# Softmax attention and a spectral filter in one kernel: some exponentials move from ScalarE to VectorE, and the instruction streams are list-scheduled anew

## The chip, the cores and the metric

The kernel runs on one core of a Trainium2 chip. The metric is the time of one execution on the device in microseconds (us), the median of several runs. An engine name in short: PE is TensorE (matmuls; PEld its weight loads), ACT is ScalarE, DVE is VectorE, POOL is GpSimd, SP is SyncE, which only issues transfers.

## What is computed

Two independent results are laid side by side in the output: multi-head attention of `A_x`, and a two-dimensional real Fourier filter of `B_x`. All inputs are bf16.

```python
B, S, D = 1, 2048, 448
H = 16; Dh = D // H                        # 16 heads of 28
q, k, v = split(x @ wqkv)                  # wqkv: D x 3D
p = softmax(q @ k.T * Dh ** -0.5)          # per head: 2048 x 2048
a = (p @ v) @ wo                           # 2048 x 448

X = rfft2(x.astype(float32))               # S x 225 complex
y = irfft2(X * (w_r + 1j * w_i), s=(S, D)) # 2048 x 448
out = concatenate([a, y], axis=-1)
```

The attention needs 16 x 2048 x 2048 exponentials, which is 1024 *units* of 128 x 512 (128 keys on the partitions, 512 queries in the columns). The Fourier transforms are products with constant tables of cosines and sines.

## The kernel before

Heads are handled in four groups of four. The 28 numbers of each head lie in a strip of 32 partitions, so the scores of different heads run in different row strips of the array at the same time, and the four products of the probabilities with V run in four column strips. A unit `u` is one head `j`, one block of 128 keys `kc`, one block of 512 queries `qc`, one group `g`. Three units make one exp of 128 x 1536. PSUM has eight banks of 512 fp32 columns: six for scores (two triples), one accumulator (`ACC`), one for all other products ("jobs").

```python
def emit_st(t):                      # scores of three units
    for u in us:
        e.matmul(bank(u % 6), kT[32*j:32*j+28, ...], qT[32*j:32*j+28, ...],
                 start=True, stop=True, tile_position=(32 * j, 0))          # L649
def emit_act(t):
    e.activation(ET[:, t % NE, 0:n], PS[:, b0:b0 + n], ACT.Exp, scale=scale) # L659
def emit_pv(u0):                     # four heads, one block of keys
    e.matmul(ACC[32*j:32*j+32, :], Vaug[:, g % 2, kc, 32*j:32*j+32],
             ET[...], start=(kc == 0), stop=(kc == 15),
             tile_position=(0, 32 * j))                                      # L670
```

`Vaug` has a column of ones beside the 28 of V, so the accumulator also holds the sums of the softmax; after 16 blocks of keys they are turned, inverted, spread and multiplied in (`finish`). Projections for the next group (L393 for q and k, L408 for v), the output product (L711) and the spectral half are jobs: lists of full-array matmuls into bank 7, each ended by a copy out of PSUM, mostly on VectorE.

```python
def s_job(h, r, b):   # along S: 8 matmuls of 112 x 512, table F1 (1024 rows)   L464
def x_job(h,sg,r,b):  # along D: 8 matmuls of 113 x 512                        L487
def zmul(b, sg, h):   # times the filter: 6 products and sums and a copy on GpSimd, 113 x 512
def w_job(q,part,b):  # the filter's tables turned on TensorE                   L534
def y_job(t, r):      # back along D: 8 matmuls of 128 x 448                    L554
def z_job(a, odd):    # back along S: 8 matmuls of 128 x 448                    L586
```

A loop of Python decides at build time in which order each engine gets its instructions; it keeps an estimate of when each engine is free (`P.free`) and emits, at each step, a scores pass if its banks are free, else a V product, else a job's next matmul. Each engine then runs its own list strictly in that order and waits on semaphores.

Of the kernel before, what the change touches and what calls it, by code (L numbers as in the profile page):

```python
# [10 lines left out]
F32 = mybir.dt.float32  # L11

_ENG = ("sp", "act", "pe", "dve", "pool")
LAT = 0.12


class Prog:

    def __init__(self, nc, sems):
        self.nc = nc
        self.streams = {e: [] for e in _ENG}
        self.sems = sems
        self.count = {name: 0 for name in sems}
        self.wm = {e: {name: 0 for name in sems} for e in _ENG}
        self.trk = {}
        self.csem = {"act": "act", "pe": "pe", "dve": "dve", "pool": "pool"}
        self.dma_sems = set(n for n in sems if n.startswith("d_"))
        self.free = {e: 0.0 for e in _ENG}  # L30
        self.dma_free = 0.0
        self.tw = {}
        self.tr = {}

# [11 lines left out]
    def _emit_waits(self, eng, reads, writes):  # L46
        waits = {}

        def add(ev):
            if ev is None:  # L50
                return
            s, v = ev
            if s in self.dma_sems:
                v = self.count[s]
            if eng == "pe" and s == "pe":
                return
            if self.wm[eng][s] >= v:
                return
            if waits.get(s, 0) < v:
                waits[s] = v  # L60
        for k in reads:
            add(self._entry(k)["w"])
# [10 lines left out]
    def _mark(self, eng, ev, reads, writes, end):  # L73
# [3 lines left out]
        for k in writes:  # L77
            en = self._entry(k)
            en["w"] = ev
            en["r"] = []  # L80
            self.tw[k] = (eng, end)

    def ready(self, eng, reads=(), writes=()):

        t = 0.0
        for k in list(reads) + list(writes):
            w = self.tw.get(k)
            if w is not None and w[0] != eng:
                t = max(t, w[1] + LAT)
        for k in writes:  # L90
            for r, e in self.tr.get(k, {}).items():
                if r != eng:
                    t = max(t, e + LAT)
        return t

    def op(self, eng, fn, reads=(), writes=(), cost=0.1, tail=0.15):
        self._emit_waits(eng, reads, writes)
        sem = self.csem[eng]
        self.count[sem] += 1
        ev = (sem, self.count[sem])  # L100
        semh = self.sems[sem]
        self.streams[eng].append(lambda e, fn=fn, semh=semh: fn(e).then_inc(semh, 1))
        start = max(self.free[eng], self.ready(eng, reads, writes))
        self.free[eng] = start + cost
        self._mark(eng, ev, reads, writes, start + cost + tail)
        return start + cost

    def dma(self, eng, fn, sem, reads=(), writes=(), kb=128, issue=0.6):
        self._emit_waits(eng, reads, writes)
# [6 lines left out]
        self.dma_free = max(self.dma_free, start + issue) + kb / 280.0  # L116
        self._mark("dma", ev, reads, writes, self.dma_free + 2.0)

# [18 lines left out]
S = 2048  # L137
# [4 lines left out]
KBN = (113, 112)  # L142


def spectral_constants():


    s = np.arange(1024)
    f1 = np.zeros((4, 128, 8, 512))
    f2 = np.zeros((8, 128, 2, 8, 128))  # L150
    for h in range(2):
        k = 2 * np.arange(512) + h
        ang = 2 * np.pi * ((s[:, None] * k[None, :]) % S) / S
        re = np.cos(ang)
        im = -np.sin(ang)
        if h == 0:
            im[:, 0] = (-1.0) ** s
        for part, m in enumerate((re, im)):
            f1[2 * h + part] = m.reshape(8, 128, 512).transpose(1, 0, 2)
            mt = m.T.reshape(4, 128, 8, 128)  # L160
            f2[:, :, part, 4 * h:4 * h + 4, :] = mt.transpose(2, 1, 0, 3)
    d = np.arange(D)
# [3 lines left out]
    t1 = np.stack([c, sn, -sn, -c]).reshape(4, 4, 112, KD).transpose(2, 0, 1, 3)  # L166
    cf = np.full(KD, 2.0)
    cf[0] = cf[224] = 1.0
    c2 = (cf[None, :] * c / (S * D)).T
    s2 = (cf[None, :] * sn / (S * D)).T  # L170
    t2 = np.zeros((128, 4, 2, D))
    for v, m in enumerate((c2, -s2, s2, -c2)):
        for b in range(2):
            t2[0:KBN[b], v, b, :] = m[KB0[b]:KB0[b] + KBN[b], :]
    return f1, f2, t1, t2


def build_kernel(nc, A_x, A_wqkv, A_wo, B_x, B_w_r, B_w_i, out):
    NG = 4
    UN = 1024  # L180
    TU = 3
    NT = (UN + TU - 1) // TU
    NE = 5
    WARM = 20
    scale = float(DH) ** -0.5
    bf16np = mybir.dt.np(BF16)

    f1, f2, t1, t2 = spectral_constants()
    cst = np.zeros((128, 3, 128), np.float32)
    cst[:, 0, :] = np.eye(128)  # L190
    cst[:, 1, :] = np.eye(128)[::-1]
    for j in range(4):
        cst[32 * j + DH, 2, j] = 1.0
    f1_h = nc.inline_tensor(f1.reshape(4 * 128, 4096).astype(bf16np), name="cst_f1")
    f2_h = nc.inline_tensor(f2.reshape(8 * 128, 2048).astype(bf16np), name="cst_f2")
    t1_h = nc.inline_tensor(t1.reshape(112, 16 * KD).astype(bf16np), name="cst_t1")
    t2_h = nc.inline_tensor(t2.reshape(128, 8 * D).astype(bf16np), name="cst_t2")
    cst_h = nc.inline_tensor(cst.reshape(128, 384).astype(bf16np), name="cst_id")

    ctx = ExitStack()  # L200
    with ctx:
        sem_names = ["pe", "act", "dve", "pool"]
        sem_names += ["d_x%d" % i for i in range(3)] + ["d_w", "d_wv", "d_wo", "d_c", "d_t1", "d_t2", "d_xb"]
        sem_names += ["d_f%d" % i for i in range(4)] + ["d_wb%d" % i for i in range(2)] + ["d_o%d" % i for i in range(4)]
# [5 lines left out]
        wst = sb("wst", [128, 4, 1344])  # L210
# [3 lines left out]
        qT = sb("qT", [128, 2, S])  # L214
        kT = sb("kT", [128, 2, S])
        Vaug = sb("Vaug", [128, 2, 16, 128])
        ET = sb("ET", [128, NE, 1536])
        oaug = sb("oaug", [128, 2, 512])
        rz = sb("rz", [128, 2, 16])
        rzrep = sb("rzrep", [128, 2, 512])  # L220
        onrm = sb("onrm", [128, NG, S])
        cid = sb("cid", [128, 3, 128])
        astg = sb("astg", [128, 4, 448])
        R1 = sb("R1", [128, 10752])
        R2 = sb("R2", [128, 8192])
        WT = sb("WT", [128, 2, 2, 2, 1024])
        Wst = sb("Wst", [128, 2, 2, 4, KD])
        FR = sb("FR", [128, 2, 4096])
        T1 = sb("T1", [128, 4, 4, KD])
        T2 = sb("T2", [128, 4, 2, 448])  # L230
        ptmp = sb("ptmp", [128, 2, 512], F32)
        Esb = sb("Esb", [128, 2, 448], F32)
        PS = ctx.enter_context(nc.psum_tensor("PS", [128, 4096], F32))
        ACC = PS[:, 3072:3584]

        xb = R1[:, 0:7168].rearrange("p (c d) -> p c d", c=16)
        xs = R1[:, 7168:10752].rearrange("p (c d) -> p c d", c=8)
        X = R1[:, 0:8192].rearrange("p (b s r k) -> p b s r k", b=2, s=2, r=2)
        Sd = R2[:, :].rearrange("p (b r k) -> p b r k", b=4, r=2)
        Y = R2[:, 0:7168].rearrange("p (t r d) -> p t r d", t=8, r=2)  # L240
        F1v = FR[:, :, :].rearrange("p i (c m) -> p i c m", c=8)
        F2v = FR[:, :, :].rearrange("p i (j r t s) -> p (i j) r t s", j=2, r=2, t=8)

        crow = [(0, 128, 0), (0, 128, 128), (0, 128, 256), (64, 128, 320)]

        xa = R2[:, 0:1792].rearrange("p (c d) -> p c d", c=4)
# [4 lines left out]
        def copy(eng, dst, src, reads, writes, cost):  # L251
            if eng == "act":
                P.op("act", lambda e: e.activation(dst, src, ACT.Copy), reads=reads, writes=writes, cost=cost)
            else:
                P.op(eng, lambda e: e.tensor_copy(dst, src), reads=reads, writes=writes, cost=cost)  # L255


        P.dma("sp", lambda e: e.dma_start(cid[:, :, :], cst_h.ap()[:, :].rearrange("p (i k) -> p i k", i=3)), "d_c", writes=["cid"], kb=96)
        P.dma("sp", lambda e: e.dma_start(xa, A_x[0][0:512, :].rearrange("(c p) d -> p c d", p=128)),
              "d_x0", writes=["xa"], kb=448)  # L260
        for lo, hi, sem, key in ((0, 896, "d_w", "w"), (896, 1344, "d_wv", "wv")):
            P.dma("act", lambda e, lo=lo, hi=hi: e.dma_start(wst[:, 0:3, lo:hi], A_wqkv[0:384, lo:hi].rearrange("(c p) k -> p c k", p=128)),
                  sem, writes=[(key, 0)], kb=0.75 * (hi - lo))
            P.dma("act", lambda e, lo=lo, hi=hi: e.dma_start(wst[64:128, 3, lo:hi], A_wqkv[384:448, lo:hi]),
                  sem, writes=[(key, 1)], kb=0.125 * (hi - lo))
        for n, lo, hi in ((1, 512, 1024), (2, 1024, 2048)):
            for c in range(4):
                dlo = crow[c][2]
                P.dma("sp", lambda e, lo=lo, hi=hi, c=c, dlo=dlo: e.dma_start_transpose(xAT[:, c, lo:hi], A_x[0][lo:hi, dlo:dlo + 128]),
                      "d_x%d" % n, reads=["xa"], writes=[("xAT", n, c // 2)] + ([("xAT", 3, c // 2)] if n == 2 else []), kb=(hi - lo) / 2, issue=1.2 * n)  # L270

        P.op("dve", lambda e: e.memset(onrm[:, 0, 0:512], 0.0), writes=["zero"], cost=0.3)
        P.op("dve", lambda e: e.memset(wk[:], 0.0), writes=["wk0", "wk"], cost=1.0)
        P.op("dve", lambda e: e.memset(wq[:], 0.0), writes=["wq0", "wq"], cost=1.0)
        P.op("pool", lambda e: e.memset(wo[:], 0.0), writes=["wo"], cost=1.6)
        for i in range(2):
            P.op("pool", lambda e, i=i: e.memset(Vaug[:, i, :, :], 0.0), writes=[("V", i, n) for n in range(4)], cost=1.9)
# [620 lines left out]
```

The softmax here doesn't subtract the row's maximum and nothing guards it: scores larger than these inputs give would overflow.

## Time and profile before

| | before |
|---|---|
| median of 3 runs | 563.34 us (560.5 to 572.84) |
| span of the profiled run | 570.4 us |
| mean granted clock of TensorE | 0.844 |
| exps on ScalarE (L659), busy | 467.3 us, 342 instructions |
| idle of ScalarE before exps | 79.0 us |
| TensorE busy / VectorE busy / GpSimd busy | 500.1 / 132.4 / 87.1 us |

The page divides the span into 40 slices and gives each engine's busy share in tenths, and the clock that TensorE was granted, also in tenths (9 is 90% or more). Groups of instructions are named by their source line (L659), engine, output and inputs. "Idle before" is the time an engine stood still just ahead of a group, with what ended the wait. A busy TensorE at half clock does half the work, so its busy time has to be read beside the clock.

### The profile page before, as it was taken

The numbers are of one execution on the slowest core, as the hardware profiler recorded it, in microseconds if no ns is written. First come the engines' busy times: TensorE is split into PE (matmuls) and PEld (weight loads), VectorE is DVE, ScalarE is ACT, GpSimd is POOL, SyncE is SP. The second block draws the span as 40 slices with busy tenths as digits, with TensorE's granted clock in tenths as the row PEclk, the third lists the DMA queues.
The fourth block names the chain that finished last, engine by engine and source line by source line (L and its number), as shares of the span: only waits on it lengthen the run. The fifth ranks groups of instructions, "written<-read, shape, count | busy, mean of one in ns | idle before, by whom it ended". The sixth has DMA issues, their size and how long they took to land.

```text
span 570.4 us, 7748 instructions
## 1 busy us (share of the span) xinstructions
PE 500.1 (88%) x3276; PEld 164.7 (29%) x3276; DVE 132.4 (23%) x218; ACT 473.6 (83%) x352; POOL 87.1 (15%) x87
## 2 busy tenths in 40 slices
PE   7699795999999999989999899999978888788786
PEld 3222232223333233333333222222222222222222
DVE  2111332212212222122211211213132122222323
ACT  2667895869999999999988579889977559899894
POOL 5038000000000000582505555000000000000000
PEclk9555755659999999999968659789999669999999
DMA  6492130000022022000000000000000011301012
GB/s 167 87 302 81 43 95 16 2 1 0 1 75 75 2 72 75 1 0 2 1 1 0 1 0 1 2 0 1 1 0 1 1 53 55 106 17 41 24 34 80
DMA packets 21394, 21.69 MB, mean 38 GB/s; under 512 B 11792, under 2 KB 19472, under 8 KB 20848
## 3 DMA queue, kind: packets, MB, share of 16 engines
q1 hardware_dynamic: 20208, 19.60, 11.8%
q10 hardware_dynamic: 960, 1.20, 0.7%
q0 software_dynamic: 192, 0.40, 0.3%
q8 instruction: 25, 0.41, 0.3%
q14 instruction: 9, 0.07, 0.1%
HBM read 15.95 MB, written 3.67 MB: 34 GB/s over the span
## 4 chain that ended last, share of the span: by engine, by line
PE 44%; ACT 28%; DMA 13%; issue 6%; DVE 6%; SPq 2%; DVEq 0%; ACTq 0%
ACT ET L659 28%; PE PS L649 11%; PE PS L670 8%; DMA Wst<-in_B_w_r_dram 6%; PE PS L554 5%; PE PS L393 4%; PE PS L487 4%; PE PS L586 3%; PE PS L408 3%; DMA Wst<-in_B_w_i_dram 3%; DMA xAT<-in_A_x_dram 3%; PE PS L464 2%; PE PS L711 1%; DMA R<-in_A_x_dram 1%; DVE R L569 1%
## 5 line engine op out<-in xcount | busy, mean ns | idle before, releaser
L659 ACT ACTIVATE ET<-PS 128x1536 bf16<-128x1536 f32 x342 | 467.3, 1611 | 79.0 <-PE PS L649 78.2
L649 PE MATMUL PS<-qT,kT 28*128 28x512 bf16 x1024 | 149.9, 435 | 26.3 <-ACT ET L659 16.0
L670 PE MATMUL PS<-ET,Vaug 128*32 128x512 bf16 x1024 | 115.4, 444 | 3.7 <-DVE Vaug L255 3.6
L649 PEld LDWEIGHTS PS<-qT,kT 28*128 28x128 bf16 x1024 | 33.6, 92 | 136.1 <-ACT ET L659 98.6
L670 PEld LDWEIGHTS PS<-ET,Vaug 128*32 128x32 bf16 x1024 | 26.5, 95 | 74.2 <-issue 68.4
L487 PE MATMUL PS<-R,T 112*113 112x512 bf16 (+1 forms) x128 | 45.6, 469 | 0.8 <-DVE Vaug L255 0.4
L518 POOL TENSOR_TENSOR ptmp<-R,WT 113x512 f32<-113x512 bf16 (+1 forms) x8 | 9.2, 1153 | 236.4 <-DVE R L500 236.4
L464 PE MATMUL PS<-FR,R 128*112 128x512 bf16 x128 | 39.8, 409 | 1.4 <-DVE R L468 0.5
L554 PE MATMUL PS<-T,R 113*128 113x448 bf16 (+1 forms) x128 | 34.7, 379 | 1.8 <-DVE R L569 0.8
L586 PE MATMUL PS<-R,FR 128*128 128x448 bf16 x128 | 35.1, 391 | 0.9 <-DVE R L569 0.5
L408 PE MATMUL PS<-wst,xAT 128*128 128x112 bf16 (+1 forms) x256 | 33.1, 242 | 2.8 <-DVE astg L598 0.8
L393 PE MATMUL PS<-xAT,wk 128*128 128x512 bf16 x64 | 25.5, 481 | 8.0 <-DMA xAT<-in_A_x_dram 5.6
L393 PE MATMUL PS<-xAT,wq 128*128 128x512 bf16 x64 | 23.3, 451 | 5.1 <-DVE astg L598 1.3
L500 DVE CAST R<-PS 113x512 bf16<-113x512 f32 (+1 forms) x16 | 11.1, 692 | 62.8 <-PE PS L487 33.5
L408 PEld LDWEIGHTS PS<-wst,xAT 128*128 128x128 bf16 (+1 forms) x256 | 18.1, 103 | 23.8 <-issue 8.8
L468 DVE CAST R<-PS 112x512 bf16<-112x512 f32 x16 | 11.1, 692 | 55.7 <-PE PS L464 55.7
L569 DVE CAST R<-PS 128x448 bf16<-128x448 f32 x16 | 10.0, 625 | 52.7 <-PE PS L554 44.1
L487 PEld LDWEIGHTS PS<-R,T 112*113 112x113 bf16 (+1 forms) x128 | 15.4, 151 | 19.5 <-issue 12.5
L255 DVE CAST Vaug<-PS 128x448 bf16<-128x448 f32 x16 | 10.0, 625 | 45.0 <-PE PS L408 45.0
L255 DVE CAST kT<-PS 128x512 bf16<-128x512 f32 x16 | 11.1, 691 | 40.2 <-PE PS L393 40.1
L534 PE MATMUL PS<-cid,Wst 128*113 128x128 bf16 (+1 forms) x64 | 10.8, 307 | 10.5 <-DMA Wst<-in_B_w_i_dram 8.7
L464 PEld LDWEIGHTS PS<-FR,R 128*112 128x112 bf16 x128 | 14.0, 133 | 17.9 <-issue 10.8
(57 smaller groups left out, 263.7 us busy)
## 6 DMA issues: line engine op xcount, KB each, us to landing
FR<-cst_f SPq DMA_DIRECT2D x4, 1024.0 KB, 8.4
FR<-cst_f SPq DMA_DIRECT2D x8, 512.0 KB, 3.6
out_dram<-astg SPq DMA_DIRECT2D x32, 112.0 KB, 1.7
R<-in_B_x_dram SPq DMA_DIRECT2D x2, 896.0 KB, 7.9
T<-cst_t SPq DMA_DIRECT2D x1, 896.0 KB, 4.7
T<-cst_t SPq DMA_DIRECT2D x1, 787.5 KB, 13.6
wst<-in_A_wqkv_dram ACTq DMA_DIRECT2D x1, 672.0 KB, 4.9
Wst<-in_B_w_r_dram SPq DMA_DIRECT2D x2, 225.0 KB, 9.9
```

Of the source, the lines that this page charges most:

```text
L255: P.op(eng, lambda e: e.tensor_copy(dst, src), reads=reads, writes=writes, cost=cost)
L393: mms.append(lambda e, M, c=c, rlo=rlo, rhi=rhi: e.matmul(M, wsb[rlo:rhi, c, g, :], xAT[rlo:rhi, c, 512 * n:512 * (n + 1)], start=(c == 0) ...
L408: mms.append(lambda e, M, c=c, rlo=rlo, rhi=rhi, kq=kq: e.matmul(M[:, 112 * kq:112 * kq + 112], xAT[rlo:rhi, c, 128 * (4 * n + kq):128 * ( ...
L464: mms.append(lambda e, M, c=c: e.matmul(M[0:112, :], src[:, c, 112 * b:112 * b + 112], F1v[:, i, c, :], start=(c == 0), stop=(c == 7)))
L468: P.op("dve", lambda e: e.tensor_copy(Sd[0:112, b, r, 512 * h:512 * h + 512], M[0:112, :]), reads=[mk], writes=[("Sd", h, r, b)], cost=0.68)
L487: mms.append(lambda e, M, ti=ti, part=part, v=v, q=q: e.matmul(M[0:kn, :], T1[0:112, v, q, k0:k0 + kn], Sd[0:112, q, part, 512 * h:512 * h ...
L554: mms.append(lambda e, M, ti=ti, sg=sg, p=p, v=v, b=b, kn=kn: e.matmul(M[:, 0:448], X[0:kn, b, sg, p, ks], T2[0:kn, v, b, :], start=(ti == ...
L569: P.op("dve", lambda e: e.tensor_copy(Y[:, t, r, :], M[:, 0:448]), reads=[mk], writes=[("Y", t, r)], cost=0.6)
L586: mms.append(lambda e, M, r=r, tt=tt, n=n: e.matmul(M[:, 0:448], F2v[:, a % 4, r, tt, :], Y[:, tt, r, :], start=(n == 0), stop=(n == 7)))
L649: ins = e.matmul(bank(u % 6), kT[32 * j:32 * j + DH, g % 2, 128 * kc:128 * (kc + 1)], qT[32 * j:32 * j + DH, g % 2, 512 * qc:512 * (qc + 1 ...
L659: P.op("act", lambda e: e.activation(ET[:, t % NE, 0:n], PS[:, b0:b0 + n], ACT.Exp, scale=scale), reads=[("B", u % 6) for u in us], writes ...
L670: ins = e.matmul(ACC[32 * j:32 * j + 32, :], Vaug[:, g % 2, kc, 32 * j:32 * j + 32], ET[:, t % NE, c0:c0 + 512], start=(kc == 0), stop=(kc ...
```

## The change

The scheduler and the spectral half are written anew; the number of scores and of probabilities is the same. The parts:

1. **Exponentials on VectorE.** For three of the 16 key blocks (`DKS = (3, 7, 11)`) the scores, scaled in k by 128 log2(e) / sqrt(28), get a bias added and are written as int16; read as bf16, such a bit pattern is a power of two whose mantissa is linear. Four patterns shifted by 32 each (a quarter of an octave), weighted by 2^(-i/4) in copies of V, are summed in the accumulator and smooth the line. The other 13 blocks stay on ScalarE. This replaces the exact exponential in these blocks by an approximation.
2. **Shared PSUM banks, list-scheduled.** Seven banks serve scores, VectorE units and jobs alike, so an exp takes three, two or one unit, as banks and probability slots are free. VectorE and GpSimd instructions go into queues and are emitted by due time.
3. **Everything but the scores in column strips.** A full-array matmul is split into four of 32 columns, so that it is of one tiling kind with the V products.
4. **Folded spectral half.** `B_x` is folded by the symmetries of cosine and sine along both axes (rows read backwards by gathers of GpSimd), so the tables have 512 rows instead of 1024 and fewer products are needed; the filter is applied in a layout that needs no turning of its tables. GpSimd does the multiplication and a part of the folding.
5. **Idle gaps of TensorE filled.** Where the schedule foresees that TensorE has nothing to do for over 0.15 us and its activity in the last 3.4 us is under 0.95, it gets products of constants whose result nobody reads; this is meant to keep its clock at the full rate.
6. **x is turned on TensorE** throughout, where before only its first quarter was and the rest came by transposing transfers.

```diff
-        ET = sb("ET", [128, NE, 1536])
+        Vs = sb("Vs", [128, 2, ND, NW - 1, 128])
+        ET = sb("ET", [128, ESL, 512])
+        TT = sb("TT", [128, NW, TSL, 512], I16)
...
+        def fill_dve(dsel):
+            for bk, (qi, b, kc, j, slot) in dsel:
+                P.defer("dve", lambda e, bk=bk, slot=slot: e.tensor_scalar(TT[:, 0, slot, :], bank(bk), BIAS, 0.0, ALU.add, ALU.max),
+                        reads=[("B", bk)], writes=[("T", slot)], busy=psum_cost(512), allow=0.8)
+                if slot % 2 == 1:
+                    for c in range(1, NW):
...
+                        P.defer("dve", lambda e, c=c, slot=slot: e.tensor_scalar(TT[:, c, slot - 1:slot + 1, :], TT[:, 0, slot - 1:slot + 1, :],
+                                                                                 SHF * c, None, ALU.add),
+                                reads=[("T", slot - 1), ("T", slot)], writes=[("T", c, slot // 2)], busy=0.336, allow=3.0, port=True)
...
+        def mm(out, lhsT, rhs, start, stop):
...
+            def cols(e):
+                m = out.shape[0]
+                for c in range(0, m, 32):
+                    c1 = min(c + 32, m)
+                    ins = e.matmul(out[c:c1], lhsT[:, c:c1], rhs, start=start, stop=stop, tile_position=(0, c))
+                return ins
...
+            if FILLER and cands and now > 20.0:
+                gap = min(cands) - now
+                if gap > FGAP and activity(now) < FACT:
...
+                        def fn(e, bk=bks[0], n=n):
+                            for h in range(0, n, 256):
+                                for c in range(4):
+                                    ins = e.matmul(PS[32 * c:32 * c + 32, 512 * bk + h:512 * bk + h + 256], cid[:, 32 * c:32 * c + 32], cid[:, 0:256],
+                                                   start=True, stop=True, tile_position=(0, 32 * c))
```

The spectral functions after the change, in short: `s_job` has 4 matmuls of 512 instead of 8, `x_job` 4 of 225, `zmul` is 12 GpSimd operations of 225 and 4 of 450 per tile of 128 rows (8 tiles), `i_job` (back along S) 4 of 512 with further folding on VectorE and GpSimd (`combine`), `y_job` (back along D) 4 of 448.

## The prediction

> **What bounds the kernel now.** I read the clock line and the busy lines of the page first, because they show that the run is not one stage but several:
>
> ```profile
> PE 500.1 (88%) x3276; PEld 164.7 (29%) x3276; DVE 132.4 (23%) x218; ACT 473.6 (83%) x352; POOL 87.1 (15%) x87
> PE   7699795999999999989999899999978888788786
> ACT  2667895869999999999988579889977559899894
> PEclk9555755659999999999968659789999669999999
> ```
>
> TensorE (PE) has the larger share, but the digits show ACT at 9 wherever PEclk is 9 and ACT at 5 to 8 wherever PEclk is 5 to 7. So I asked for busy time by stretches cut at the clock changes (PE, PEld, DVE, ACT, POOL, then the granted clock):
>
> ```profile
> 20.00:132.00 112.00, 97.02 (x563) 30.53 (x561) 25.04 (x39) 81.27 (x58) 17.81 (x18) 0.56 0.28 76
> 132.00:290.00 158.00, 145.24 (x1082) 52.70 (x1079) 38.26 (x61) 158.00 (x119) 30.66 (x28) 1.00 0.08 28
> 290.00:376.00 86.00, 81.62 (x443) 23.90 (x442) 14.80 (x24) 66.30 (x49) 30.45 (x28) 0.70 0.00 1
> 426.00:500.00 74.00, 60.82 (x399) 19.32 (x399) 16.45 (x27) 52.79 (x39) 0.00 (x0) 0.85 0.13 42
> ```
>
> At full clock ScalarE is busy 158.00 of 158 us: the exps are the bound there. At a clock of 0.56 it is busy 81 of 112: TensorE is the bound there. The list of waits (us in total, times, longest) confirms what ScalarE waits for:
>
> ```profile
> ACT ET L659 <- PE PS L649: 78.2, 68, 6.3
> ```
>
> So the span is: first exp at 13.8 us, exps busy 467.3, idle before exps 79.0, and about 10.4 after the last, in sum 570.5 (span 570.4).
>
> Two costs come from the timeline. In 132 to 290 us, 119 exps of 128x1536 take 159.96 us, 1.344 each; a lone one lasts 1.45 and a lone ACTIVATE of 128x512 0.597, so (1.45 - 0.597)/1024 = 0.833 ns per column, and 1.344 - 1.280 = 0.064 fixed in a stream. On PE:
>
> ```profile
> 200.12 0.39 PE L649 MATMUL PS<-qT,kT 28*128 28x512 bf16 x3 [0.44 <-ACT ET L659]
> 200.44 0.10 PEld L670 LDWEIGHTS PS<-ET,Vaug 128*32 128x32 bf16 x4 [0.23 <-issue]
> ...
> 320.83 0.61 PE L649 MATMUL PS<-qT,kT 28*128 28x512 bf16 x3
> 321.37 0.27 PEld L487 LDWEIGHTS PS<-R,T 112*113 112x113 bf16 x2 [0.44 <-issue]
> ```
>
> From a scores pass to the next kind of product 0.32 us pass at clock 1.0 and 0.54 at 0.5. Of 0.32, some 0.216 is streaming (consecutive L464 matmuls: seven from 202.11 and 203.22 show about 0.22 each) and about 0.105 the change of tiling.
>
> [...] from 320 to 344 us PE is busy 4.00 of 4.00 in each slice and still at 0.50, so a busy row alone does not bring the clock back. [...] The trace has 692 ns for 128x512 fp32 from PSUM [...] and 246 ns for a 64x336 bf16 SBUF copy [...]. [...] the new code orders such instructions by semaphore (`port=True`).
>
> **The change, part by part** (counts are from the two compiled instruction lists).
>
> *Exps.* Three of 16 key blocks go to VectorE, so ScalarE keeps 832 of 1024 units of 512. They come as 108 x 1536, 243 x 1024 and 22 x 512: 108x1.344 + 243x0.917 + 22x0.491 = 145 + 223 + 11 = 379 us, against 467. Equal-sized triples would give 373; the sharing of banks costs 6.
>
> *VectorE.* It gains 192 PSUM reads of 128x512 to int16. One row is 692 ns, but in a stream starts lie closer: 561.85 to 562.39 for 448 columns, 0.54 [...]; so 0.607, in sum 117. Then 288 shifts of 128x1024 [...] 0.34, in sum 98. What it had stays in kind: about 79 evictions for attention (47 us), 16 reciprocals (5), 26 output rows (14), 56 spectral evictions (33), two fold chunks in fp32 (12), scaled V, xAT and starts (about 13). Sum 340 us. The old rz broadcast and the transposes of W (16 x 0.69) go away.
>
> *TensorE.* Scores stay 1024 in some 377 passes: 81 us. There are 742 changes of tiling: 78. PV is 13 + 3x4 = 25 groups per block instead of 16: 400 x 0.216 = 86 (before 55). Projections: 120 groups x 0.216 = 26, V 256 groups at 0.105 (16 took 1.69) = 27. The spectral half shrinks, since folding by symmetry leaves transforms of 512 in place of 1024: s 64 groups, i 68, x 64 of 225, y 64 of 448, so 14 + 15 + 6 + 12 = 47, against 128 x 4 = 512 full matmuls before, about 104 (256 x 0.216 + 256 x 0.19). Output product 12, normalisation and transposes 15. Sum 372 at full clock. Filler: 1216 matmuls of 256 columns, four at a time, 304 x 0.107 = 32. In all 404.
>
> *GpSimd.* The products by W and the folds grow: 96 operations of 225 at about 0.62 and 32 of 450 at about 1.1 (rows of before: 448 bf16 in 1035 ns, 512 in 1152 to 1269), two fold chunks 24, combining 19, gathers and starts some 30: about 170 us against 87.
>
> *On the path:* start 14 (x, wqkv and the first two projections are as before), 379 of exps, and a tail. After the last scores pass the list still has 7 rows of the spectral output and 12 of attention's, 75 groups x 0.19 = 14 us, plus one normalisation chain: I take 17. Sum 410 us with ScalarE never idle. Idle before exps: at full clock before had 0 of 158 us and (50 - 48.4) + (60 - 56.4) = 5.2 of 110, together 2%. Now VectorE (340) and PE (404 with filler) are nearly as full as ScalarE, all streams are in order and placed by estimated durations, and S has two or three units of lead instead of three plus three. I choose 7%, 27 us. **Predicted: 437 us**, 126 less than 563.
>
> **Rivals.**
> (a) *The clock still falls.* Fillers are placed only where the schedule foresees a gap; a real wait of PE on a semaphore is not filled. For it: before fell to half clock from slices in which PE was 78 to 90% busy. Against it: PE has 404 us of work in 437, and the fall came in stages with long full-array spectral passes. At the old mean clock of 0.844, 372/0.844 = 441, plus start and tail 31: about 470.
> (b) *VectorE becomes the bound.* [...] VectorE would need 570 and the kernel about 590. For it: no int16 row exists in before. [...]
> (c) *GpSimd holds the inverse transform back.* The list has the x products between score units 413 and 499 and the first inverse ones at unit 813: 314 units, about 120 us, for 8 tiles of 11.8 us = 94 [...]. PE runs in order, so a late GpSimd stops the exps too: +10 to +30, about 450 to 465.
> (d) *Little is gained, for the exps were hidden behind PE anyway.* Were PE the bound everywhere, its added PV (31 us) and changes would eat the gain. Against it: the 158 us at full clock.
>
> **Range and chances.** The floor of my sum is 410. (c) or part of (a) leads to 450 to 480. Range 412 to 482. Only (b), or the clock at half for most of the run, brings it near 563: faster 0.94, same 0.02, slower 0.04.
>
> **What would show it.** PEclk at 9 in nearly all slices and mean clock above 0.95: filler right. ACT exps near 379 busy, idle before them near 27 and not 79. `TT<-TT` rows near 0.43 us (0.34 start to start), `TT<-PS` 0.69; 1.2 us would be rival (b). Waits of PE on GpSimd's `R1a` before L443 of more than 10 us would be rival (c). The sum is wrong if exps wait mostly on PE at full clock (schedule too tight), or if the start or the tail is longer than 14 and 17.

## The result and the profile after

| | before | after |
|---|---|---|
| median | 563.34 us (568.09 with a fourth run) | 463.2 us (461.3 to 464.2) |
| ratio | 1 | 0.8255 (95% interval 0.820 to 0.831) |
| span of the profiled run | 570.4 us | 460.5 us |
| mean granted clock of TensorE | 0.844 | 0.978 |
| exps on ScalarE: busy, idle before them | 467.3, 79.0 us | 388.6, 35.4 us |
| first exp starts, last exp to the end | 13.8, 10.8 us | 13.7, 23.4 us |

The ratios, and the medians of the experiments, leave out runs more than 1.5% above the fastest of their kernel; the profiled run of before (by its span that of 572.84 us) is one of these, some 11 us above the middle of the two that stay (560.5 and 563.34), so that the profiles differ by more than the times do. The prediction was 437 us, range 412 to 482. On a later chip the same kernel took 492.8 us; that is the second finding below, and it belongs to the result.

The page of after, busy line, slices and the three groups that the prediction named (busy, mean ns, then idle before):

```profile
PE 424.8 (92%) x7484; PEld 164.9 (36%) x7484; DVE 348.2 (76%) x731; ACT 395.2 (86%) x383; POOL 165.5 (36%) x203
PE   7889899988998899998998899999899999999994
DVE  2856699999989397676768788968668788996361
ACT  2687569999999899995899999999999999999911
PEclk9999999999999899995899999999999999999998
L934 ACT ACTIVATE ET<-PS 128x1024 bf16<-128x1024 f32 (+2 forms) x373 | 388.6, 1153 | 35.4 <-PE PS L905 33.1
L944 DVE TENSOR_SCALAR TT<-PS 128x512 int16<-128x512 f32 x192 | 129.5, 685 | 32.8 <-PE PS L905 31.0
L949 DVE TENSOR_SCALAR TT<-TT 128x1024 int16<-128x1024 int16 x288 | 105.9, 421 | 12.8 <-POOL ptmp L546 11.5
```

PEclk is 9 nearly everywhere, and ACT mostly so. Its dents lie at the start, in the fifth and sixth slices (46 to 69 us), in the nineteenth (207 to 219), the only place where PEclk falls to 5, and in the tail. The mean of 1153 ns hides three widths (1536, 1024 and 512 columns), as "+2 forms" says.

The timeline of several engines around the two holes (start, us, engine, line, [idle before <- releaser]) shows what the dents are:

```profile
61.37 24.64 ACT L934 ACTIVATE ET<-PS 128x1024 bf16<-128x1024 f32 x23 [9.08 <-PE PS L905]
...
53.41 4.14 POOL L546 TENSOR_TENSOR R1b<-wst 128x896 bf16<-128x896 f32 x2 [2.69 <-DVE TT L949]
57.65 0.20 DVE L516 TENSOR_SCALAR Vs<-Vaug 128x128 bf16<-128x128 bf16 x1 [1.93 <-POOL R1b L546]
...
207.31 0.76 DVE L949 TENSOR_SCALAR TT<-TT 128x1024 int16<-128x1024 int16 x2 [2.72 <-POOL ptmp L546]
208.73 0.94 PE L443 MATMUL PS<-T,R 113*32 113x225 bf16 x16 [1.84 <-DVE TT L944]
```

From 46.6 to 57.6 us GpSimd folds `B_x` in two pairs of steps of 2.1 us each. By `port=True` the code makes such steps take turns, by semaphore, with VectorE's scaled copies of V and its shifts. That they are needed was assumed when the code was written; what the chip does without them is measured in E10 (a shift of 1752 ns instead of 420). So the copies and shifts stand in line behind GpSimd (1.93 us before the copy at 57.65 us), the V products that need them come late, and the scores, and so the exps, behind those: 9.08 us. Shortly before 206 us GpSimd starts on the filter; a shift waits 2.72 us, PE then waits 1.84, and its clock falls. The stretch in one line (engines as before, then the clock):

```profile
200.00:220.00 20.00, 18.16 (x269) 6.78 (x261) 12.48 (x28) 13.85 (x14) 13.89 (x20) 0.70 0.09 19
```

PE is busy 18.16 of 20 us and ScalarE only 13.85. From 210 to 220 us, at a clock of 0.50, PE is busy throughout and ScalarE 6.1 of 10 us: at half clock a busy PE didn't keep the exps fed. Four V products in strips take 0.62 us there and twelve 1.50 (217.72 and 218.12 us), against 0.39 and 0.82 at full clock (46.13 and 46.35 us), so each further four add 0.44 us in place of 0.21. The wait of 1.84 us was followed by about 12 us of half clock; the filler is placed at build time and can't answer a wait nobody foresaw.

### The profile page after: what moved, and what is told of

Read it like the earlier page. It is cut to its first block, busy times and chain, and to the rows that moved or that the text cites. A ratio compares the mean times of both kernels' runs of the same rounds, so it can differ in the third digit from the quotient of the medians.

```text
span 460.5 us, 16944 instructions
## 1 busy us (share of the span) xinstructions
PE 424.8 (92%) x7484; PEld 164.9 (36%) x7484; DVE 348.2 (76%) x731; ACT 395.2 (86%) x383; POOL 165.5 (36%) x203
## 4 chain that ended last, share of the span: by engine, by line
PE 41%; ACT 23%; DVE 16%; POOL 8%; DMA 6%; issue 6%; SPq 0%; DVEq 0%; ACTq 0%; POOLq 0%
ACT ET L934 22%; PE PS L443 13%; PE PS L1001 13%; PE PS L905 13%; DVE TT L944 5%; DVE TT L949 4%; POOL R1b L541 3%; DMA out_dram<-wst 2%; DMA R1a<-in_B_x_dram,idx 2%; DVE onrm L546 2%; PE PS L1333 2%; DMA wst<-in_A_wqkv_dram 2%; POOL ptmp L546 1%; POOL R1b L546 1%; POOL wst L546 1%
## 5 line engine op out<-in xcount | busy, mean ns | idle before, releaser
L934 ACT ACTIVATE ET<-PS 128x1024 bf16<-128x1024 f32 (+2 forms) x373 | 388.6, 1153 | 35.4 <-PE PS L905 33.1
L944 DVE TENSOR_SCALAR TT<-PS 128x512 int16<-128x512 f32 x192 | 129.5, 685 | 32.8 <-PE PS L905 31.0
L949 DVE TENSOR_SCALAR TT<-TT 128x1024 int16<-128x1024 int16 x288 | 105.9, 421 | 12.8 <-POOL ptmp L546 11.5
L1001 PE MATMUL PS<-ET,Vaug 128*32 128x512 bf16 x832 | 83.4, 394 | 4.4 <-ACT ET L934 3.6
L1333 PE MATMUL PS<-cid 128*32 128x256 bf16 x1216 | 56.0, 275 | 3.6 <-DVE qT L495 1.3
L1001 PE MATMUL PS<-TT,Vs 128*32 128x512 bf16 x576 | 40.3, 384 | 0.1
L546 POOL TENSOR_TENSOR ptmp<-ptmp,R1b 128x450 f32<-128x450 f32 x32 | 31.6, 1010 | 14.1 <-DVE TT L949 10.0
L1333 PEld LDWEIGHTS PS<-cid 128*32 128x32 bf16 x1216 | 27.1, 95 | 26.7 <-issue 7.7
L546 POOL TENSOR_TENSOR ptmp<-R1a 128x225 f32<-128x225 bf16 (+2 forms) x36 | 25.1, 716 | 15.7 <-DVE TT L949 12.8
L443 PE MATMUL PS<-T,R 112*32 112x448 bf16 (+4 forms) x512 | 28.0, 323 | 2.1 <-DVE TT L944 1.8
L546 POOL TENSOR_TENSOR ptmp<-ptmp 128x225 f32<-128x225 f32 x32 | 18.1, 582 | 17.2 <-DVE TT L949 9.2
```

The source lines that it names most:

```text
L443: ins = e.matmul(out[c:c1], lhsT[:, c:c1], rhs, start=start, stop=stop, tile_position=(0, c))
L546: P.defer(eng, lambda e: e.tensor_tensor(out, a, b, op), reads=reads, writes=writes, busy=c, allow=allow, port=True, after=after)
L934: P.op("act", lambda e: e.activation(dst, src, ACT.Exp, scale=ESC), reads=[("B", i) for i in o], writes=[("E", p + k) for k in range(n)], ...
L944: P.defer("dve", lambda e, bk=bk, slot=slot: e.tensor_scalar(TT[:, 0, slot, :], bank(bk), BIAS, 0.0, ALU.add, ALU.max), reads=[("B", bk)], ...
L949: P.defer("dve", lambda e, c=c, slot=slot: e.tensor_scalar(TT[:, c, slot - 1:slot + 1, :], TT[:, 0, slot - 1:slot + 1, :], SHF * c, None, ...
L1001: ins = e.matmul(ACC[32 * j:32 * j + 32, :], lh, rhs, start=first, stop=last, tile_position=(0, 32 * j))
```

## The experiments

Twelve runs on three chips; the very first measurement was on a chip that isn't known. E1 to E8 ran on one chip, E9 and E10 on a second, E11 and E12 on a third. The first eight texts use 463 us as their yardstick, and letters in a text belong to that text. E4, E5 and E8 have a second edit, of the tail: an output copy meant for ScalarE goes to the queue for VectorE if its buffer isn't free yet. What it does by itself was not measured.

| run | what differs from the changed kernel | us | yardstick | difference |
|---|---|---|---|---|
| E9 | nothing, second chip | 467.0 | | |
| E10 | no semaphore waits for the turns of `port=True` | 505.9 | 467.0 | +39 |
| E11 | nothing, third chip | 492.8 | | |
| E12 | eight output buffers, third chip | 484.9 | 492.8 | -8 |
| E6 | the same, first chip | 485.0 | 492.8 | -8 |
| E1 | no filler | 500.1 | 492.8 | +7 |
| E2 | these turns in neither plan nor semaphores | 531.9 | 492.8 | +39 |
| E3 | the kernel before, with filler | 567.4 | before, 560.6 | +7 |
| E4 | full-array jobs in place of strips | 491.7 | 492.8 | -1 |
| E5 | no exps on VectorE | 534.0 | 492.8 | +41 |
| E7 / E8 | folding all on GpSimd / all on VectorE | 485.6 / 483.5 | 492.8 | -7 / -9 |

E1 to E8 are held against 492.8 although that was measured on another chip. What carries this: the same version with eight buffers gave 485.0 on the first chip and 484.9 on the third, and both show the trait described next. Differences under some 5 us between the two chips should still not be leaned on.

### The chip: E9 and E11

Of the variants on the first chip, E6 to E8 had come out some 20 us above 463, with pauses of TensorE that no edit explained. The unaltered kernel was therefore run again, twice.

> The changed kernel itself, unaltered, run again beside the others. If the starved stretches of the matrix engine that the last variants showed (13 to 25 us and 201 to 221 us, some 0.7 us between groups of four small matmuls, while the DMA engines are near full) belong to those variants' own instruction streams, this run repeats 460 to 465 us with a clock of 0.97 to 0.98 and none of them. If they belong to the conditions of the run, it gives 480 to 490 us with a clock of 0.94 to 0.95, waits of ScalarE on something the profile can't name of 10 us or more, and then the last three variants are the same as the changed kernel and not 20 us worse.

> The changed kernel once more, unaltered, beside the version with eight output buffers. If the starved stretches belong to the chip that a run meets (the earlier variants all ran on another chip than its last repeat), then this run and the one beside it show the same thing: either both are starved at 13 to 25 us and come out at 480 to 490 and 475 to 485 us, or neither is, at 460 to 468 and 454 to 463 us. If they belong to each kernel's instruction streams, this one is 460 to 468 us without them.

E9 gave 467.0 us (464.0 to 469.9), ratio to before 0.830 (0.822 to 0.839). E11 gave 492.8 (489.9 to 495.4), even over the 480 to 490 that its text named for a chip with the pauses, ratio 0.882 (0.868 to 0.896). The kernel before took 562.9 us on the second chip (four runs) and 555.2 on the third (two runs), so it is not slower there; it has no gathers, on which more below. Timeline of PE, first E9, then E11:

```profile
13.84 0.39 PE L905 MATMUL PS<-qT,kT 28*128 28x512 bf16 x4 [0.69 <-ACT qT L492]
14.16 0.97 PE L443 MATMUL PS<-wv,xAT 112*32 112x112 bf16 x64
```

```profile
13.66 0.67 PE L443 MATMUL PS<-wv,xAT 112*32 112x112 bf16 x40
14.53 0.24 PE L443 MATMUL PS<-wv,xAT 112*32 112x112 bf16 x2 [0.20 <-issue]
15.25 0.28 PE L443 MATMUL PS<-wv,xAT 112*32 112x112 bf16 x5 [0.48 <-issue]
```

The same 64 small matmuls take 0.97 us in one go on the second chip and over 5 us on the third. "issue" means that PE waited for nothing the profile shows. Busy time in two stretches (PE, PEld, DVE, ACT, POOL, clock), E9 and then E11:

```profile
14.00:40.00 26.00, 23.56 (x557) 12.07 (x553) 17.90 (x38) 18.89 (x18) 21.22 (x15) 1.00 0.57 188
200.00:240.00 40.00, 38.11 (x651) 14.88 (x648) 28.45 (x60) 32.60 (x33) 24.93 (x39) 0.83 0.05 11
```

```profile
14.00:40.00 26.00, 18.63 (x239) 8.46 (x227) 11.96 (x25) 10.36 (x10) 9.99 (x10) 0.67 0.55 182
200.00:240.00 40.00, 24.18 (x396) 9.37 (x384) 16.52 (x34) 18.46 (x20) 16.46 (x19) 0.70 0.26 70
```

ScalarE loses 8.5 us in the first stretch and 14.1 in the second, 22.7 of the 26 by which the spans differ. In the second it is not PE alone that stands still. Timeline of E11, where "remote" is a releaser that the profile can't name:

```profile
210.42 0.69 DVE L944 TENSOR_SCALAR TT<-PS 128x512 int16<-128x512 f32 x1 [8.64 <-remote]
210.48 1.02 ACT L934 ACTIVATE ET<-PS 128x1024 bf16<-128x1024 f32 x1 [7.88 <-remote]
211.17 0.28 PE L443 MATMUL PS<-cid,oaug 128*32 128x4 bf16 x16 [7.79 <-DVE TT L944]
```

For some 7 us PE, VectorE and ScalarE all rest, while GpSimd and SyncE go on issuing transfers. Over the whole run ScalarE waits 18.1 us before exps on "remote" and 9.8 at the start on products that come late; its waits on scores are as in E9 (33.4 and 32.5 us).

In both stretches GpSimd issues gathers (13 to 23 us, and 200 to 219 in E11). The pauses follow the gathers wherever a variant on a chip with pauses has them: 162 to 182 us in E5, 171 to 191 in E7, 207 to 227 in E8. From E8's timeline:

```profile
218.46 0.66 PE L1001 MATMUL PS<-TT,Vs 128*32 128x512 bf16 x3 [0.75 <-issue]
...
219.82 0.94 POOL L541 DMA_INDIRECT R1b<-in_B_w_r_dram,idx  x1 [0.30 <-issue]
220.59 0.65 PE L1001 MATMUL PS<-TT,Vs 128*32 128x512 bf16 x3 [1.46 <-issue]
221.07 0.95 POOL L541 DMA_INDIRECT R1b<-in_B_w_i_dram,idx  x1 [0.30 <-issue]
```

So it isn't the variants' code but the chip (or the occasion: only the first chip was met twice, with pauses both times), and it happens while gathers are issued. On the second chip the same gathers (14 to 24 and 186 to 206 us) go with no pause of 0.3 us or more. Busy DMA engines alone are not the reason: in E11 their share is 1.1 from 10 to 14 us without a pause of this kind, and 0.15 to 0.27 from 210 to 222 us with pauses. That the gathers are the cause isn't shown, since a version without them wasn't tried; nor is it known why two chips of three react.

### The turns of VectorE and GpSimd: E10 and E2

E2 takes the turns of `port=True` out of both the plan and the semaphores, E10 out of the semaphores alone:

```diff
-        self._emit_waits(eng, reads, writes, self.port[1] if port and self.port[0] not in (None, eng) else None)
+        self._emit_waits(eng, reads, writes, None)                  # E10
...
     def op(self, eng, fn, reads=(), writes=(), busy=0.1, check=True, port=False):
+        port = False                                                # E2, and the same in defer
```

> The changed kernel without the semaphore order between VectorE's and GpSimd's SBUF instructions (data dependences stay). Theory A (the exclusive order is what the exps lose time to: VectorE waits for GpSimd 11.5 us ahead of the shifts and GpSimd for VectorE over 60 us, and the gap of 9 us at 52 us comes from it): exps idle 15 to 22 us instead of 35, time 445 to 453. Theory B [...]: operations get longer instead, time 458 to 468.

> Keeps the plan that counts GpSimd and VectorE as taking turns [...], and leaves out only the semaphore waits that enforce the turns; the instruction list of every engine is otherwise the same. If what cost 50 to 70 us in the run without order was the overlap itself on the chip (VectorE's shift rows 0.56 us instead of 0.42), this one loses most of it too: shift rows above 0.48 us, 490 to 530 us. If it was the plan (GpSimd's steps put side by side with the shifts so that the products that carry the exps come late), this one stays within 15 us of the changed kernel run beside it, with shift rows of 0.42 to 0.46 us.

Both lost 39 us, E10 against the same kernel on its own chip; E2's text had allowed for 445 to 468 us and was far off. Since E10 keeps the plan and loses as much, the overlap on the chip is enough to explain the loss. Groups of E10 within 236 to 292 us, where GpSimd does the filter, and below them the same of E9:

```profile
L934 ACT ACTIVATE ET<-PS 128x1024 bf16<-128x1024 f32 (+1 forms) x28 | 29.3, 1053 | 27.5 <-PE PS L905 27.2
L949 DVE TENSOR_SCALAR TT<-TT 128x1024 int16<-128x1024 int16 x15 | 25.5, 1752 | 0.0
L546 POOL TENSOR_TENSOR ptmp<-ptmp,R1b 128x450 f32<-128x450 f32 x20 | 20.1, 1032 | 0.0
```

```profile
L934 ACT ACTIVATE ET<-PS 128x1024 bf16<-128x1024 f32 (+1 forms) x53 | 56.1, 1195 | 1.1 <-PE PS L905 1.0
L949 DVE TENSOR_SCALAR TT<-TT 128x1024 int16<-128x1024 int16 x42 | 15.1, 420 | 2.9 <-POOL ptmp L546 2.8
L546 POOL TENSOR_TENSOR ptmp<-ptmp,R1b 128x450 f32<-128x450 f32 x15 | 14.9, 1011 | 7.4 <-DVE TT L949 6.0 <-DVE Vs L516 1.4
```

Without the semaphores GpSimd runs back to back (idle 0.0) and hardly slows, 1032 ns against 1011. A shift takes 1752 ns instead of 420; three in a row took 7.27 us. VectorE's reads of scores from PSUM (L944) stay as they were, 682 ns against 685. ScalarE gets through 28 exps instead of 53. Part of this comes by way of the clock: PE, which waits for the shifts, has a clock of 0.50 in this stretch, against 1.00 in E9. So the 32.0 us that GpSimd's filter rows (`ptmp`) wait for shifts in after are the cheap side of the bargain. Whether the 1752 ns are a wait of the shift or a slower shift, the trace doesn't tell. The whole-run mean (573 ns in E10) hides this; the stretch shows it.

### Exps on VectorE: E5

```diff
-DKS = (3, 7, 11)
+DKS = ()
```

> The changed kernel with all 1024 units of exps on ScalarE (no key block on VectorE); folded spectral half, shared banks, strips and filler stay. By the stream cost, 1024 units in triples and pairs need 460 to 475 us of ScalarE. Theory A (ScalarE is the bound and the rest of the change only keeps it fed): start 14 + 470 + idle 20 + tail 20, time 515 to 530, so the exps on VectorE bring some 55 us of the 100 and the rest of the change 45. Theory B (the exps on VectorE bring little[...]): 480 to 500.

```profile
L934 ACT ACTIVATE ET<-PS 128x1536 bf16<-128x1536 f32 (+2 forms) x413 | 467.4, 1379 | 41.4 <-remote 20.7
```

All exps back on ScalarE cost 467.4 us busy, as before the change, and the kernel 534.0 (531.3 to 535.0): 41 us over E11. The whole gain on chips with the pauses is 62 to 68 us (492.8 against 555.2 for the kernel before on E11's chip, 560.4 on E5's). The other 21 to 27 us belong to the rest of the change; of its parts only the filler and the strips were tried alone (below), the shared banks and the folded spectral half were not. E5 came out some 4 us over the upper figure expected, which had left out the pauses (20.7 us of "remote"). ScalarE's load falls by 79 us (467.4 to 388.4 in E11) and only 41 arrive: E11 idles 63.0 us before exps against 41.4, and its tail is longer (23.4 us against 9.3; E5 also has the edit of the tail).

### The filler: E1 and E3

E1 sets `FILLER` to `False`. E3 gives the kernel before a filler of zero weights, added to the accumulator while it is open:

```diff
+                        ins = e.matmul(ACC[32 * c:32 * c + 32, 0:256], zw[:, 0:32], cid[:, 0:2, :],
+                                       start=False, stop=False, tile_position=(0, 32 * c))
```

> The changed kernel (463 us, mean clock 0.978) with no products of constants: its gaps on TensorE stay empty, all else is scheduled by the same rules. Theory A (the filler is what keeps the clock up): the mean clock falls to about 0.85 to 0.90, exps wait 40 us longer, time 490 to 510. Theory B (the dense schedule keeps the clock up by itself, and 304 groups of filler at 0.107 us only stand in the way): clock above 0.95 and time 450 to 463.

> The kernel before, with one part of the change alone: where its own schedule has a gap of over 0.15 us, four column-strip products of 256 columns with zero weights are added into the accumulator (588 groups, some 63 us of TensorE at full clock); the sum is not changed by them. Theory A (before's loss was the clock alone): mean clock from 0.844 to above 0.95, idle before exps from 79 to 15 to 30 us, time 510 to 530. Theory B (its long full-array jobs at half clock stop the exps and filler cannot lift the clock there): clock below 0.9, time 550 to 600.

Slices and exps of E1, then of E3:

```profile
PEclk9759957799999998559987986779765899999999
L934 ACT ACTIVATE ET<-PS 128x1024 bf16<-128x1024 f32 (+2 forms) x366 | 389.0, 1162 | 83.1 <-PE PS L905 53.3
```

```profile
PEclk9559996999999999999999999999966799999899
L661 ACT ACTIVATE ET<-PS 128x1536 bf16<-128x1536 f32 x342 | 474.8, 1462 | 66.8 <-PE PS L651 63.9
```

E1's clock is 0.863 against 0.948 in E11, and its exps wait 83.1 us against 63.0; the end came only 7 us later, because its other list left less work behind the last exp (14.4 us against 23.4). The filler does keep the clock up, as meant, but it is worth a fifth of the 33 us that rival (a) had put on a falling clock (470 less 437), or half if the tails were equal (7 + 9 us, an estimate); on a chip without pauses it was not tried. E3 shows the converse: the clock rose to 0.937 (before has 0.844 in its profile, 0.863 and 0.874 in the two runs that count beside E3) and the time did not fall, 567.4 us against 560.6. Exps wait 66.8 us there instead of 79.0, but take 474.8 instead of 467.3, and 102.7 us of filler are new on PE. A higher clock bought with filler is not the gain.

### Full-array jobs: E4

E4 builds every job as full-array matmuls (`full=True`), so that the column strips of part 3 fall away.

> The changed kernel with projections, spectral products and output product as single full-array matmuls instead of four column strips (fewer instructions: 4952 matmuls instead of 7484). Theory A (the strips save changes of tiling between jobs and V products, each 0.105 us): 150 to 250 more changes, time 470 to 490. Theory B (a change of tiling between full and strips costs nothing, only that from row strips to others does): time 458 to 468.

491.7 us against 492.8: no difference. Cutting jobs into strips neither bought nor cost time. The change of tiling itself is in E4's timeline: after four V products (strips) another product in strips starts 0.23 us later, a full-array job or a scores pass 0.33. So a change costs about 0.10 us, between full array and strips too, as the prediction had estimated (0.105); TensorE had room for it.

### Where the folding is done: E7 and E8

```diff
-FOLD = ((0, "pool"), (1, "dve"), (2, "pool"), (3, "dve"))
+FOLD = ((0, "dve"), (1, "dve"), (2, "dve"), (3, "dve"))    # E8 (and the edit of the tail); all "pool" in E7
```

> The changed kernel with all four chunks of the fold on GpSimd (before: two of four on VectorE). Theory A (VectorE is overfull from 40 to 105 us, busy 20 of 20): it loses 12 us of work there, exps idle less in this stretch, time 450 to 458. Theory B (the gap of 9 us at 52 us comes from GpSimd's 2 us instructions [...]): 24 us more of such instructions, time 465 to 475.

> The changed kernel with all four chunks of the fold on VectorE. Theory A (VectorE overfull): 12 us more on it, time 468 to 478. Theory B (long GpSimd instructions [...]): none of them before unit 400, the gap at 52 us is gone, time 450 to 458.

ScalarE of E8 around the place of the 9.08 us hole:

```profile
43.48 2.40 ACT L934 ACTIVATE ET<-PS 128x1536 bf16<-128x1536 f32 x2 [1.89 <-PE PS L905]
51.48 1.45 ACT L934 ACTIVATE ET<-PS 128x1536 bf16<-128x1536 f32 x1 [1.73 <-PE PS L905]
```

With no folding on GpSimd there is no such hole, only five waits of 4.5 us together from 41 to 54 us; in E11, which has the pauses too, it is 9.10 us at 74 us. So the hole comes with GpSimd's folding. E8 idles 54.6 us before exps against 63.0; its tail is 4.6 us longer, and its profiled span 5.4 us shorter (482.7). E7 keeps the hole (8.19 us) and yet gives 485.6: its exps idle more, 72.7 us, but only 9.3 us are left after the last one. Both gains are near the limit of a comparison between chips.

### The tail: E6 and E12

```diff
-        astg = wflat[:, 0:1792].rearrange("p (s d) -> p s d", s=4)
+        astg = wflat[:, 0:3584].rearrange("p (s d) -> p s d", s=8)
```

> The changed kernel with eight staging slots for output rows instead of four. In the tail ScalarE waits 9.4 us and VectorE 4.3 us for output transfers to leave their slots. Theory A (the slots set the tail): the tail after the last exp falls from 23 to about 17 us, time 455 to 458. Theory B (the transfers themselves, 1.8 us each one after another, set the end): same within 1.5 us, 461 to 464.

> Eight output buffers for the attention half in place of four, as before. Unstarved if the chip decides: 454 to 463 us, some 5 us under the changed kernel beside it, all of it behind the last exp (17 to 18 us instead of 23). Starved again while the changed kernel beside it is not, if the instruction streams decide: 482 to 487 us, three waits of ScalarE on something unnamed, 24 us together.

Waits of ScalarE's output copies in after (total, times, longest) and, second, in E12:

```profile
ACT wst L1073 <- DMA out_dram<-wst: 9.4, 3, 3.9
ACT wst L1073 <- PE PS L443: 5.6, 2, 5.3
```

```profile
ACT wst L1073 <- DVE wst L1076: 6.0, 2, 4.3
ACT wst L1073 <- PE PS L443: 3.0, 3, 1.7
```

With four buffers the copies wait for transfers to leave, 9.4 us; with eight that line is gone. From the end of the last exp to the end of the span it is 23.4 us in E11 and 17.1 in E12. On the same chip the times are 492.8 and 484.9, a ratio of the means of 0.985 (0.977 to 0.993). **This version beats both kernels** where it was run; it met only chips with the pauses.

## Why the prediction was right in kind and 26 us short

- **What the gain is.** Right: exps leave ScalarE, and the clock holds. ScalarE's exps and its idle time before them fall by 122.3 us (467.3 + 79.0 to 388.6 + 35.4); the longer tail takes 12.6 back (10.8 to 23.4), and the span falls by 109.9. E5 shows the exps' part of it; the parts that cut the idle time are not told apart.
- **The reading of before.** ACT at 9 wherever PEclk is 9, and lower where it is lower, holds for most slices, not for all: the sixth has ACT 9 at PEclk 5, and slices 30, 31, 35 and 38 have ACT 7 or 8 at PEclk 9. E3, where a higher clock brought no time, is a warning against reading it as the whole cause.
- **Clock and filler.** 0.978, as stated (above 0.95). PE is busy 424.8 us instead of 404. What a falling clock costs was over-estimated: 7 us in E1, where it fell to 0.863, not 33.
- **Rival (b), VectorE bound.** Refuted: shifts take 421 ns a row and 0.335 us start to start ("1.09" for three in a row), not the 1.2 us of the rival; PSUM reads take 685 ns; VectorE is busy 348.2, stated 340. Rows of before lead to both figures: VectorE's copies between bf16 tiles in SBUF took 246 ns for 64x336 and 191 for 64x112, 0.25 ns a column, casts out of PSUM 692 for 128x512 and 625 for 128x448, 1.05 ns a column. A shift of 1024 columns is then an estimated 0.41 us at the first rate and 1.23 at the second, from the start to the end of one row. That int16 shifts would run like the bf16 copies was my assumption; the 421 ns bear it out.
- **Exps, 379 us: measured 388.6.** The widths came as counted (108, 243, 22). The stream cost was applied to all; but an exp that starts after a wait takes 1.02 us for 1024 columns, in a stream 0.917 (eight in 7.44). The timeline has 43 fresh starts, some 4.5 us; the other 5 are not assigned.
- **Idle before exps, 27 us: measured 35.4.** The 7% was a choice, and one mechanism was missing from it: 9.1 us at the fold and 6.6 at the filter's start (2.6 at the wait, 4.0 at the half clock after it, to 221 us) begin where VectorE waits its turn for GpSimd. I had read the semaphores of these turns as a cost on GpSimd's side alone. That these are the 8.4 us too many isn't shown, since the 27 had no parts.
- **Rival (c), GpSimd late.** The engine was right, the place wrong. Nothing waits 10 us for the inverse transform; VectorE waits for its turn with GpSimd instead (11.5 us before shifts, by the page). That 94 us of GpSimd's work might not fit into 120 was my estimate.
- **Tail, 17 us: measured 23.4.** The sum counted PE's work and one normalisation chain, not that output copies wait for one of four buffers to drain. With eight it is 17.1. The order of the last work counts as well: E7 has four buffers and a tail of 9.3.
- **Start.** 14 stated, 13.7 measured.

The three terms, 9.6 + 8.4 + 6.4, make up 24.4 of the 26; most of the rest is that the sum is a span and the prediction a time (460.5 and 462.26 us in the profiled run). Not foreseen at all was the chip: at 492.8 us the kernel would have been outside the range, and that the first measurement met a chip without the pauses was luck.

## What to carry to other kernels

When 16-bit rows of VectorE between SBUF tiles and work of GpSimd, like the shifts and the filter here, share a stage, try to order them by semaphore and to cut GpSimd's steps short: here order was worth 39 us of the kernel's time, and steps of 2.1 us at the wrong place went with a hole of 9 (shorter steps were not tried). Count the buffers that the last outputs need, not only the work behind the last exp. And run a new version's control on the same chip as its variants: 26 us between chips looked like a whole batch of failed edits.

## What the runs showed of the hardware that I had not expected

- On two of three known chips TensorE pauses between a few matmuls each while GpSimd issues indirect gathers (0.30 to 2.17 us in E5, from 166 to 185 us), and TensorE, VectorE and ScalarE stood still together for some 7 us (E11, waits of 7.79, 8.64 and 7.88 us); on one chip (E9) they didn't, with the same instructions.
- With GpSimd working back to back, a shift of 128x1024 int16 took 1752 ns on average instead of 420, while GpSimd's own steps of 128x450 took 1032 ns instead of 1011 (E10 and E9, 236 to 292 us).
- A single 1.84 us wait of TensorE was followed by about 12 us at half clock with TensorE busy all the time (after, 209 to 221 us: busy 12.00 of 12.00 us, clock 0.50).
- A change of tiling, full array to column strips included, cost about 0.10 us of TensorE at full clock (starts 0.33 us apart instead of 0.23 in E4).
